# Converting float64 weight slabs in pairs of 1024 columns in a packed-attention and MLP kernel

## The chip, the cores and the metric

One Trainium2 chip, one of its cores. The metric is the device time of one execution, in microseconds (us); the profile's span runs from the first to the last instruction inside it. Engines are named as in the profile: PE is TensorE (PEld its weight loads), DVE is VectorE, ACT is ScalarE, POOL is GpSimd, SP is SyncE, whose queue (SPq) issues almost all DMAs.

## The reference

Three stages in a row, in float32. The inputs arrive as they were drawn, and the weight matrices of the two MLPs arrive as float64.

```python
p_packed = sm_attn(p, k, v)             # 32 packed queries per head, 8 x 8 heads, 576 keys, width 64
out = sm_attn(q, p_packed, p_packed)    # 576 queries on 32 packed rows
x = transposed to (4608, 512)
xn = x / rms * rms_g
x = (silu(xn @ w_gate) * (xn @ w_val)) @ w_out      # 512 -> 1536 -> 512
h = x @ w_in
y = np.maximum(0.01 * h, h) @ w_out2                # 512 -> 2048 -> 512
```

## The kernel before, in words

**Three stretches.** The head (the slots with negative numbers in the tables) does the attention of the first two batches. Then 96 steps of the first MLP follow: a step is one group of 256 hidden columns (six groups), one of two batches of a pair and one half of the batch's 576 tokens. A step runs the products g and v (line 924, `gv`), the SiLU and its product with v (line 938, `hidden`), and four products y of the step before it (line 947, `y_out`). The attention of later batches, weight conversions and other small work hang between them in slots, four to a step. At last the second MLP runs in five blocks of tokens by a fast product scheme (seven products in place of eight, twice over); its weights and their sums lie in DRAM by then.

**Weights.** PE takes each matrix as two parts, a rounded one and the rest of it (hi and lo), so each product is three matmuls. The gate and value weights are first multiplied with the packed attention rows by `fold` (line 883): four small matmuls per batch into a PSUM tile `pwps`, a copy of it on ACT (hi, `pw`, line 170) and a subtraction on DVE (lo, line 178). The next g and v products read `pw`.

**Conversion.** A float64 slab of 128 rows and 512 columns is made float32 by `convert` (line 694): an absolute value on ACT (line 704), then on DVE a clamp (707), a shift (713), the sign bits (724) and the low word (730). All of it runs on raw words. For the 24 slabs of gate and value weights (named `w`) the result stays as it is. For the 12 slabs of `w_out` (named `wo`, the intermediate `cvwo`) and the 32 of the second MLP (`w2`, the intermediate `cvw`) an ACT copy and a POOL subtraction split it into hi and lo. That is 68 conversions. Each converted slab is also stored to DRAM for the later batch pairs, by a store that is issued when the next conversion has been written (`flush_store`).

**Buffers.** `raw_tile` (line 773) holds raw slabs. The tag `wraw` (the slabs `w` and later `w2`) and the tag `w2` (the slabs `wo`) have two buffers each, one slab per buffer. Slabs `w2`, `w3` and `wo1` borrow room from tiles that are not yet in use. The intermediates have two buffers (`CVB`). The SP instruction that loads a slab is issued when the slab that was in its buffer has been read by line 730.

**Order.** The tables ONE, TWO, SPLITW, SPLITO, FOLD0, FOLD, SPLITA and WARM give each piece of work a slot. The conversions of the second MLP start at step 25 and come every 1.6 steps. The framework then sets the order on every engine by its own simulated timeline; what stands in an engine's queue runs in that order, and an instruction that has to wait holds all behind it.

Of the kernel before, what the change touches and what calls it, by code (L numbers as in the profile page):

```python
# [59 lines left out]
SPLITA = (-18, -20,)  # L60
WBUFS = 8
HEAD = 2
OWN = 1
HOLD = 2
# [5 lines left out]
CVB = 2  # L70
# [4 lines left out]
WARM = ([-85, 5], [-53, 2], [-41, 10], [-22, 1],)  # L75
# [3 lines left out]
def pack_attention_moe_kernel(  # L79
# [21 lines left out]
    P = 128  # L101
# [24 lines left out]
    w_dram = dram.tile([NFG * KT, P, 512], F32, name="w_dram")  # L126
# [567 lines left out]
    def convert(raw64, hl, name, whole=False, lay=None, plain=None):  # L694

        hiw, low = raw64[:, :, 1], raw64[:, :, 0]
        n = raw64.shape[1]
        st = {}

        def begin():  # L700
            c = st["c"] = (
                hl if whole else cvt.tile([P, n], F32, tag="conv", bufs=CVB, name="cv" + name)
            )
# [24 lines left out]
        def tail():  # L728
# [47 lines left out]
    NW = NFG * KT  # L776

    def load_w(i):
        if i < NW:
            fg, kt = i // KT, i % KT  # L780
            if i in (2, 3):
                t = mlpa.tile([P, 2, 512, 2], U32, tag="pw1", bufs=2, name=f"w{i}")[:, 0]
            else:
                t = raw_tile(f"w{i}")
            for x, w in enumerate((w_gate, w_val)):
                nc.sync.dma_start(
                    out=t[:, x * G * P : (x + 1) * G * P, :].rearrange("p f w -> p (f w)"),
                    in_=w[kt * P : kt * P + P, fg * G * P : (fg + 1) * G * P].bitcast(U32),
                )
# [23 lines left out]
    def load_wo(i):  # L813
        if i < NF1:
            if i == 1:
                t = mlpa.tile([P, 2, 512, 2], U32, tag="pw0", bufs=2, name=f"wo{i}")[:, 0]
            else:
                t = raw_tile(f"wo{i}", "w2")
            nc.sync.dma_start(
                out=t.rearrange("p f w -> p (f w)"), in_=w_out[i * P : i * P + P, :].bitcast(U32)  # L820
            )
            wo["r", i] = t

    def split_wo(i):
        if i < NF1:
            until(lambda: ("r", i) in wo)
            t = mlpb.tile([P, 2, 512], F32R, tag="wo", bufs=4, name=f"wo{i}")
            convert(wo.pop(("r", i)), t, f"wo{i}")

            def done():  # L830
                wo["s", i] = t
                flush_store()
                stores.append((wo_dram[i], t))
                if i >= 1:
                    load_wo(i + 1)

            after(done)
        elif i < NPAIR * NF1:
            t = mlpb.tile([P, 2, 512], F32R, tag="wo", bufs=4, name=f"wo{i}")
# [647 lines left out]
```

## Time and profile before

| | |
|---|---|
| median of 3 runs | 1608.43 us (1606.33 to 1608.69) |
| the profiled execution | 1609.27 us |
| its span | 1607.5 us |
| PE busy | 1533.7 us (95%) |
| DVE busy | 1115.1 us (69%), 2026 instructions |
| ACT busy | 762.5 us (47%), 1390 instructions |
| POOL busy | 600.3 us (37%) |
| mean granted TensorE clock | 0.985 |

Shares of busy time are means over stretches that differ much: PE is busy for 83 of the first 120 us, for 200 of the next 210, and nearly all of the last 700. So the views by stretch, the waits and the chain that ended last say more than the table. A matmul that reads a PSUM or SBUF tile late shows as idle time of PE with the engine that released it.

### The profile page before, as it was taken

Reading aid. Unit: us, or ns where it says so; the run is one execution under the profiler, and the core shown is the slowest. Engines: PE = TensorE matmul, PEld = TensorE weight load, DVE = VectorE, ACT = ScalarE, POOL = GpSimd, SP = SyncE. Lnnn points to the kernel's source line nnn. Section 1 sums busy time; section 2 is a strip of 40 time slices with the busy share of each in tenths; the row PEclk is TensorE's granted clock in tenths of the full one; section 3 lists DMA queues with packets and bytes.
Section 4 is the critical chain, followed back from the end, with each engine's and each line's share of the span. In section 5 each row is a group of like instructions: output and inputs, shape, how many; then the busy total and the mean of one; then the engine's idle time right before and its main releaser. Section 6 shows DMA issues by size and latency. Waiting matters only on the chain.

```text
span 1607.5 us, 29455 instructions
## 1 busy us (share of the span) xinstructions
PE 1533.7 (95%) x10754; PEld 1353.8 (84%) x10754; DVE 1115.1 (69%) x2026; ACT 762.5 (47%) x1390; POOL 600.3 (37%) x415
## 2 busy tenths in 40 slices
PE   4789999999999999999999999999999999999998
PEld 3558778888888888898999988888888888888998
DVE  7787997566766757879667549646854783596475
ACT  3365454464445554456434246336524652463453
POOL 1124334443524524365124463065208503710530
PEclk7999999999999999999999999999999999999999
DMA  9664562375556744559775666797787769777887
GB/s 273 211 196 148 186 206 88 129 237 176 185 190 210 246 144 148 201 181 351 244 249 207 228 203 203 212 291 203 203 260 241 206 201 288 203 202 227 279 252 209
DMA packets 219455, 342.22 MB, mean 213 GB/s; under 512 B 21168, under 2 KB 120496, under 8 KB 219312
## 3 DMA queue, kind: packets, MB, share of 16 engines
q1 hardware_dynamic: 199856, 330.90, 65.2%
q10 hardware_dynamic: 19456, 9.44, 2.2%
q8 instruction: 86, 1.41, 0.4%
q14 instruction: 57, 0.47, 0.1%
HBM read 266.86 MB, written 73.40 MB: 212 GB/s over the span
## 4 chain that ended last, share of the span: by engine, by line
PE 66%; DVE 16%; DMA 8%; ACT 4%; issue 3%; POOL 1%; SPq 1%; ACTq 0%; DVEq 0%; POOLq 0%
PE o L153 21%; PE h L153 20%; PE y L153 10%; PE g L153 5%; PE v L153 5%; DMA w<-in_moe_w_in_dram 3%; DVE y_acc L963 2%; PE pwps L901 1%; DVE sg L940 1%; DVE pw L178 1%; PE xp L577 1%; DMA k<-in_k_dram 1%; DVE cvw L707 1%; PE s L250 1%; DVE cvw L724 1%
## 5 line engine op out<-in xcount | busy, mean ns | idle before, releaser
L153 PE MATMUL o<-gh,pc 128*128 128x480 f32 (+1 forms) x1120 | 322.7, 369 | 0.0
L153 PE MATMUL y<-hh,wo 128*128 128x288 f32 x1536 | 276.3, 302 | 15.2 <-DVE pw L178 7.1
L153 PE MATMUL h<-yh,pc 128*128 128x480 f32 (+1 forms) x1120 | 278.3, 369 | 0.8 <-DVE y_acc L963 0.5
L153 PEld LDWEIGHTS y<-hh,wo 128*128 128x128 f32 x1536 | 225.4, 190 | 42.4 <-DVE pw L178 9.4
L178 POOL TENSOR_TENSOR hl<-sg,hh 128x576 fp32r<-128x576 f32 x96 | 147.1, 1533 | 299.4 <-ACT hh L170 267.1
L153 PEld LDWEIGHTS h<-yh,pc 128*128 128x128 f32 x1120 | 207.5, 188 | 27.5 <-issue 0.9
L153 PEld LDWEIGHTS o<-gh,pc 128*128 128x128 f32 x1120 | 208.6, 188 | 26.0
L178 DVE TENSOR_TENSOR gl<-g,gh 128x480 fp32r<-128x480 f32 (+1 forms) x280 | 178.9, 657 | 63.5 <-ACT gh L170 56.9
L170 ACT ACTIVATE gh<-g 128x480 fp32r<-128x480 f32 (+1 forms) x280 | 160.5, 587 | 128.8 <-PE o L153 72.8
L153 PE MATMUL o<-gl,pc 128*128 128x480 f32 (+1 forms) x560 | 206.3, 369 | 0.0
L1311 POOL TENSOR_TENSOR b6h<-b6h,b5h 128x480 f32<-128x480 f32 (+1 forms) x40 | 59.2, 1481 | 354.2 <-ACT b5h L170 267.7
L963 DVE TENSOR_TENSOR y_acc<-y_acc,y 128x288 f32<-128x288 f32 x320 | 139.4, 446 | 66.3 <-PE y L153 65.3
L153 PE MATMUL y<-hl,wo 128*128 128x288 f32 x768 | 165.2, 298 | 1.0 <-POOL hl L178 1.0
L153 PE MATMUL h<-yl,pc 128*128 128x480 f32 (+1 forms) x560 | 161.5, 369 | 0.0
L153 PE MATMUL g<-ath,pw 128*128 128x288 f32 x768 | 150.9, 306 | 3.7 <-ACT sg L1251 3.4
L153 PE MATMUL v<-ath,pw 128*128 128x288 f32 x768 | 148.6, 305 | 4.6 <-DVE sg L940 4.6
L153 PEld LDWEIGHTS g<-ath,pw 128*128 128x128 f32 x768 | 115.9, 188 | 24.9 <-issue 10.5
L153 PEld LDWEIGHTS y<-hl,wo 128*128 128x128 f32 x768 | 124.8, 191 | 2.3 <-POOL hl L178 2.3
L1305 POOL TENSOR_TENSOR g<-g,g 128x480 f32<-128x480 f32 (+1 forms) x80 | 117.0, 1462 | 23.9 <-ACT g L1295 18.8
L153 PEld LDWEIGHTS v<-ath,pw 128*128 128x128 f32 x768 | 117.0, 190 | 10.2 <-DVE sg L940 6.5
L153 PEld LDWEIGHTS o<-gl,pc 128*128 128x128 f32 x560 | 105.1, 188 | 13.1
L153 PEld LDWEIGHTS h<-yl,pc 128*128 128x128 f32 x560 | 104.3, 188 | 13.1
(162 smaller groups left out, 2443.9 us busy)
## 6 DMA issues: line engine op xcount, KB each, us to landing
pc<-s_dram SPq DMA_DIRECT2D x320, 256.0 KB, 3.0
pc<-w_dram SPq DMA_DIRECT2D x240, 256.0 KB, 3.0
w<-w_dram SPq DMA_DIRECT2D x72, 256.0 KB, 4.1
wo<-wo_dram SPq DMA_DIRECT2D x36, 512.0 KB, 5.2
w_dram<-w2s SPq DMA_DIRECT2D x32, 512.0 KB, 4.8
s_dram<-ss SPq DMA_DIRECT2D x32, 512.0 KB, 6.3
v<-in_v_dram SPq DMA_DIRECT2D x16, 576.0 KB, 5.2
y_dram<-y_acc SPq DMA_DIRECT2D x32, 288.0 KB, 2.5
```

Source lines behind the costliest of these rows:

```text
L153: mm = nc.tensor.matmul(ps, lhsT=lh if a == "h" else ll, rhs=rh if b == "h" else rl, start=start and i == 0, stop=stop and i == n - 1,)
L170: nc.scalar.activation(out=o, in_=i, func=AF.Copy, scale=scale)
L178: eng.tensor_tensor(out=o, in0=a, in1=hi.bitcast(F32), op=ALU.subtract)
L250: nc.tensor.matmul(t[:, k_, :CH], lhsT=left[:, j].rearrange("p h k -> p (h k)"), rhs=right[:, c * CS : (c + 1) * CS, j, :], start=j == 0, ...
L577: nc.tensor.matmul(xp[:, k_, :CH], lhsT=Pm[:, 2 * x : 2 * x + 2, :].rearrange("p h d -> p (h d)"), rhs=st["AT"][:, c * CS : (c + 1) * CS, ...
L707: nc.vector.tensor_scalar(out=c, in0=c, scalar1=DBL_MIN, scalar2=DBL_MAX, op0=ALU.max, op1=ALU.min)
L724: nc.vector.scalar_tensor_tensor(out=cu, in0=hiw, scalar=0xC0000000, in1=cu, op0=ALU.bitwise_and, op1=ALU.bitwise_or)
L901: return nc.tensor.matmul(ps[32 * h : 32 * h + 32], lhsT=lpw[2 * (n // NFG) + bb][rs, 2 * u + h // 2, c : c + 32], rhs=w[h // 2][rs], star ...
L940: nc.vector.tensor_tensor(out=hf, in0=sg, in1=vps[:, :, :CH], op=ALU.mult)
L963: pace[:] = [nc.vector.tensor_tensor(out=ya, in0=ya, in1=pv, op=ALU.add).ins]
L1305: eng.tensor_tensor(out=o, in0=a, in1=b, op=ALU.subtract)
L1311: return eng.tensor_tensor(out=o, in0=a, in1=b, op=ALU.add)
```

## The change

Two slabs are converted as one: 34 conversions of 1024 columns in place of 68 of 512. The raw tile becomes a pair, and each raw tag, the intermediates (`CVB`) and the split tiles of the second MLP keep one buffer of twice the size. So the buffers hold the same bytes, and a load of the next pair with the same tag waits for the last DVE operation on the pair before it, save for the first two pairs of each kind, of which one borrows room as before. The copies to hi and the subtractions to lo stay at 512 columns, two of each for a pair. Loads of `w` and `wo` are the same DMAs as before, in fours and twos; a pair of `w2` comes by one DMA of 1 MB. A pair of gate and value weights is stored and fetched again as one. The tables get new slots; those of the conversions have half as many entries.

```diff
-SPLITW = (-68, -58, -59, -57, -12, -6, -1, -1, 4, 6, 12, 13, 21, 29, 29, 29, 37, 38, 44, 42, 48, 50, 55, 56,)
-SPLITO = (-56, -65, 1, 7, 26, 29, 33, 41, 49, 53, 67, 71,)
-FOLD0 = (-38, -36, 3, -1,)
+SPLITW = (-67, -58, -37, -1, 0, 11, 21, 28, 36, 43, 47, 53,)
+SPLITO = (-56, 2, 26, 34, 49, 67,)
+FOLD0 = (-38, -38, 6, 0,)
-WBUFS = 8
+WBUFS = 4
-HOLD = 2
+HOLD = 1
-CVB = 2
+CVB = 1
...
-    def convert(raw64, hl, name, whole=False, lay=None, plain=None):
-
-        hiw, low = raw64[:, :, 1], raw64[:, :, 0]
-        n = raw64.shape[1]
+    def convert(raw, name, whole=None, halves=()):
+
+        raw = raw.rearrange("p k f w -> p (k f) w")
+        hiw, low = raw[:, :, 1], raw[:, :, 0]
+        n = raw.shape[1]
...
-            if not whole:
-                if lay:
-                    nc.sync.dma_start(out=plain, in_=c)
-                    hi, lo, c = lay(hl, c)
-                else:
-                    hi, lo = hl[:, 0, :], hl[:, 1, :]
-                act_copy(hi, c)
-                sub(nc.gpsimd, lo, c, hi)
+            for k_, (to, plain) in enumerate(halves):
+                ck = c[:, 512 * k_ : 512 * k_ + 512]
+                if plain is not None:
+                    nc.sync.dma_start(out=plain, in_=ck)
+                hi, lo, ck = to(ck)
+                act_copy(hi, ck)
+                sub(nc.gpsimd, lo, ck, hi)
...
-    def raw_tile(name, tag="wraw", bufs=2):
-        return cvt.tile([P, 512, 2], U32, tag=tag, bufs=bufs, name=name)
+    def raw_tile(name, tag="wraw"):
+        return cvt.tile([P, 2, 512, 2], U32, tag=tag, bufs=1, name=name)
...
                 stores.append((w_dram[i], t))
-                if i >= 2:
-                    load_w(i + 2)
+                if i == 0:
+                    load_w(2)
+                elif i >= 2:
+                    load_w(i + 1)
...
+            if i == 0:
+                load_wo(2)
+            elif i >= 2:
+                load_wo(i + 1)
...
     def load_w2(i):
-        if i < 32:
+        if i < 16:
             t = raw_tile(f"w2{i}")
-            nc.sync.dma_start(out=t.rearrange("p f w -> p (f w)"), in_=w2_src(i)[0].bitcast(U32))
+            to = t.rearrange("p k f w -> p k (f w)")
+            nc.sync.dma_start(out=to, in_=w2_src(i).bitcast(U32))
             w2q[i] = t
...
-    for j in range(32):
-        convs.setdefault(CONV0 + int(j * CONV), []).append(j)
+    for j in range(16):
+        convs.setdefault(CONV0 + int(2 * j * CONV), []).append(j)
```

**ACT at the first folds of group 1.** Here `w7` and `w8` before, and `w3` and `w4` in the change (`w3` holds the old `w6` and `w7`, `w4` the old `w8` and `w9`), are the first operations of conversions; `pw` are the hi copies of the folds. Before:

```order
L704 ACTIVATE w7_726<-w7_694 128x512
L584 ACTIVATE sq011_804<-xp011_0_805 128x288
L584 ACTIVATE sq011_804<-xp011_1_806 128x288
L704 ACTIVATE w8_837<-w8_723 128x512
L170 ACTIVATE pw01_736<-pwps001_811 128x512
L170 ACTIVATE pw11_849<-pwps101_850 128x512
L170 ACTIVATE pw10_847<-pwps100_848 128x512
```

And in the change:

```order
L584 ACTIVATE sq011_782<-xp011_0_783 128x288
L584 ACTIVATE sq011_782<-xp011_1_784 128x288
L170 ACTIVATE pw11_810<-pwps101_811 128x512
L170 ACTIVATE pw10_808<-pwps100_809 128x512
L170 ACTIVATE pw11_810<-pwps111_833 128x512
L170 ACTIVATE pw10_808<-pwps110_832 128x512
L707 ACTIVATE w4_717<-w4_695 128x1024
```

The conversion that stood ahead of the folds (`w8`) now stands behind all four copies of group 1, and `w7` has gone forward with its pair (`w3`, eleven rows above the first `pw11`).

**DVE ahead of the folds of group 2.** `sg` is the product of the SiLU with v, `pw` the lo part of a fold. Before, with the pair of slabs `w13` and `w14` (`w14` in the second raw buffer):

```order
L730 SCALAR_TENSOR_TENSOR w13_1521<-w13_1111,w13_1521 128x512
L940 TENSOR_TENSOR sg011_1278<-sg011_1278,v011_1288 128x576
L707 TENSOR_SCALAR w14_1531<-w14_1531 128x512
L730 SCALAR_TENSOR_TENSOR cvwo5_1552<-wo5_1438,cvwo5_1552 128x512
L713 TENSOR_SCALAR w14_1531<-w14_1531 128x512
L724 SCALAR_TENSOR_TENSOR w14_1531<-w14_1308,w14_1531 128x512
L730 SCALAR_TENSOR_TENSOR w14_1531<-w14_1308,w14_1531 128x512
L178 TENSOR_TENSOR pw21_1346<-pwps201_1347,pw21_1346 128x512
```

And in the change, where `w6` is the old `w12` and `w13`, and `w7` the old `w14` and `w15`:

```order
L733 SCALAR_TENSOR_TENSOR w6_1239<-w6_987,w6_1239 128x1024
L727 SCALAR_TENSOR_TENSOR cvwo2_1378<-wo2_285,cvwo2_1378 128x1024
L968 TENSOR_TENSOR sg011_1216<-sg011_1216,v011_1226 128x576
L733 SCALAR_TENSOR_TENSOR cvwo2_1378<-wo2_285,cvwo2_1378 128x1024
L710 TENSOR_SCALAR w7_1424<-w7_1424 128x1024
L716 TENSOR_SCALAR w7_1424<-w7_1424 128x1024
L178 TENSOR_TENSOR pw21_1286<-pwps201_1287,pw21_1286 128x512
```

Three operations stand between the last one on the pair `w6`, which frees the only raw buffer, and the first one on the pair `w7`, which is loaded into it.

**ACT among the conversions of the second MLP.** `w2s` is the hi copy at the end of a conversion, `cvw` the absolute value that begins one. Before:

```order
L170 ACTIVATE w2s6_4771<-cvw26_4772 128x4x128
L584 ACTIVATE sq141_4841<-xp141_0_4842 128x288
L584 ACTIVATE sq141_4841<-xp141_1_4843 128x288
L170 ACTIVATE lpw5_4852<-tp50_4849,g_sb_115 128x64 x2
L704 ACTIVATE cvw28_5163<-w28_5002 128x512
```

And in the change:

```order
L170 ACTIVATE w2s5_5357<-cvw25_5358 128x4x128 x2
L1279 ACTIVATE sg1011_5499<-g1011_5478 128x576
L170 ACTIVATE hh1010_5431<-sg1010_5395 128x576
L170 ACTIVATE e160_5451<-s160_1_5454 128x9x32
L170 ACTIVATE e160_5451<-s160_0_5453 128x9x32
L707 ACTIVATE cvw26_5674<-w26_5372 128x1024
```

In both, the load that the `cvw` row reads is issued when DVE has done the last operation of the conversion whose `w2s` copy stands first; the number of operations between is four in both, and the change has two copies of 512 columns in front of them.

## Rows read from the trace of the kernel before

**Rows 1.** Busy time by stretch: us, PE, PEld, DVE, ACT, POOL, clock, DMA share, GB/s.

```profile
0.00:120.00 120.00, 83.00 (x608) 60.38 (x608) 93.16 (x180) 55.42 (x101) 22.80 (x25) 0.89 0.74 226
80.00:120.00 40.00, 32.71 (x240) 23.95 (x238) 33.62 (x60) 26.28 (x47) 10.15 (x7) 1.00 0.61 196
120.00:330.00 210.00, 199.82 (x1894) 174.31 (x1900) 162.96 (x327) 105.39 (x185) 88.63 (x60) 0.98 0.48 154
330.00:750.00 420.00, 405.22 (x3747) 360.68 (x3731) 303.19 (x594) 218.80 (x383) 180.37 (x127) 0.99 0.60 200
900.00:1608.00 708.00, 699.47 (x3360) 620.54 (x3360) 444.20 (x727) 318.76 (x596) 260.56 (x176) 1.00 0.77 231
```

**Rows 2.** Chain that ended last, in two windows of the head: start, us, what.

```profile
37.29 7.58 DMA k<-in_k_dram
44.95 4.63 DMA wo<-in_moe_w_out_dram
...
by line: DMA w<-in_moe_w_val_dram 12.6%; DVE w L730 10.7%; DVE w L724 9.6%; issue 8.3%; DVE pw L178 7.2%; DVE w L713 6.4%; PE y L153 6.1%; DVE qT L497 5.1%; DVE sg L940 5.1%; DVE sm L536 4.8%; PE s L250 3.8%; PE g L153 3.0%; PE xp L577 2.9%
96.63 3.28 DMA w<-in_moe_w_val_dram
```

**Rows 3.** PE waits, 330 to 750 us: for whom, us in total, times, longest.

```profile
PE y L153 <- DVE pw L178: 6.1, 7, 2.2
```

**Rows 4.** ACT waits for raw slabs of the second MLP, 330 to 750 us.

```profile
ACT cvw L704 <- DMA w<-in_moe_w_in_dram: 37.2, 12, 5.5
ACT cvw L704 <- DMA w<-in_moe_w_out_dram: 22.3, 11, 3.9
```

**Rows 5.** DVE in order of time, independent operations: start, us.

```profile
133.25 0.42 DVE L707 TENSOR_SCALAR cvwo<-cvwo 128x512 f32<-128x512 f32 x1
133.59 0.42 DVE L707 TENSOR_SCALAR w<-w 128x512 f32<-128x512 f32 x1
136.53 0.68 DVE L724 SCALAR_TENSOR_TENSOR cvwo<-wo,cvwo 128x512 uint32<-128x512 uint32 x1
137.13 0.68 DVE L724 SCALAR_TENSOR_TENSOR w<-w,w 128x512 uint32<-128x512 uint32 x1
139.54 0.75 DVE L940 TENSOR_TENSOR sg<-sg,v 128x576 f32<-128x576 f32 x1
```

**Rows 6.** All engines in order of time, one conversion whose operations follow each other.

```profile
98.24 0.69 DVE L724 SCALAR_TENSOR_TENSOR w<-w,w 128x512 uint32<-128x512 uint32 x1
98.97 0.69 DVE L730 SCALAR_TENSOR_TENSOR w<-w,w 128x512 uint32<-128x512 uint32 x1
100.10 0.43 SPq L786 DMA_DIRECT2D w<-in_moe_w_val_dram  x1
```

**Rows 7.** Groups by form: busy us, mean ns of one | idle before.

```profile
L343 DVE STREAM_TRANSPOSE kT<-k 128x1152 f32<-128x1152 f32 x16 | 21.6, 1348 | 4.7 <-DMA k<-in_k_dram 4.7
L551 DVE STREAM_TRANSPOSE AT<-A 128x576 f32<-128x576 f32 x16 | 12.3, 770 | 4.9 <-POOL A L542 4.6
L704 ACT ACTIVATE cvw<-w 128x512 f32<-128x512 f32 x32 | 21.5, 672 | 63.7 <-DMA w<-in_moe_w_in_dram 37.2 <-DMA w<-in_moe_w_out_dram 22.3 <-POOL wo L178 2.4
L170 ACT ACTIVATE w2s<-cvw 128x512 fp32r<-128x512 f32 x32 | 20.2, 631 | 36.1 <-DVE cvw L730 35.7
L178 POOL TENSOR_TENSOR wo<-cvwo,wo 128x512 fp32r<-128x512 f32 x12 | 15.9, 1328 | 34.2 <-ACT wo L170 34.2
```

**Rows 8.** All engines in order of time, 30 to 51 us.

```profile
30.75 1.51 PE L422 MATMUL pp<-v,a1T 96*32 96x64 f32 x48 [3.32 <-DMA v<-in_v_dram]
37.95 0.47 DVE L430 SCALAR_TENSOR_TENSOR Pm<-pp,rin,mask 128x256 f32<-128x256 f32 x1
50.37 0.43 DVE L707 TENSOR_SCALAR cvwo<-cvwo 128x512 f32<-128x512 f32 x1 [2.83 <-ACT cvwo L704]
```

**Rows 9.** DMA issues: KB each, median us to landing; windows 88 to 330 and 330 to 750 us.

```profile
w<-in_moe_w_val_dram SPq DMA_DIRECT2D x17, 256.0 KB, 3.5
w<-in_moe_w_in_dram SPq DMA_DIRECT2D x14, 512.0 KB, 4.9
```

More of the change, by code (lines that the diff above doesn't have):

```diff
@@ L701, in begin @@
             c = st["c"] = (
[L702 removed]
+                cvt.tile([P, n], F32, tag="conv", bufs=CVB, name="cv" + name)
+                if whole is None
+                else whole.rearrange("p k f -> p (k f)")
             )
@@ L771, in until @@
             drain(1)
-    def raw_tile(name, tag="wraw", bufs=2):
-        return cvt.tile([P, 512, 2], U32, tag=tag, bufs=bufs, name=name)
-    NW = NFG * KT
+    def raw_tile(name, tag="wraw"):
+        return cvt.tile([P, 2, 512, 2], U32, tag=tag, bufs=1, name=name)
+    NW = NFG * KT // 2
     def load_w(i):
         if i < NW:
-            fg, kt = i // KT, i % KT
-            if i in (2, 3):
-                t = mlpa.tile([P, 2, 512, 2], U32, tag="pw1", bufs=2, name=f"w{i}")[:, 0]
+            fg, k0 = i // 2, i % 2 * 2
+            if i == 1:
+                t = mlpa.tile([P, 2, 512, 2], U32, tag="pw1", bufs=2, name=f"w{i}")
             else:
                 t = raw_tile(f"w{i}")
[L785 to L789, printed above, removed]
+            for k_ in range(2):
+                kt = k0 + k_
+                for x, w in enumerate((w_gate, w_val)):
+                    nc.sync.dma_start(
+                        out=t[:, k_, x * G * P : (x + 1) * G * P, :].rearrange("p f w -> p (f w)"),
+                        in_=w[kt * P : kt * P + P, fg * G * P : (fg + 1) * G * P].bitcast(U32),
+                    )
             wq["r", i] = t
@@ L813, in load_wo, with wo_tile, done, fetch_wo @@
     def load_wo(i):
-        if i < NF1:
+        if i < NF1 // 2:
             if i == 1:
-                t = mlpa.tile([P, 2, 512, 2], U32, tag="pw0", bufs=2, name=f"wo{i}")[:, 0]
+                t = mlpa.tile([P, 2, 512, 2], U32, tag="pw0", bufs=2, name=f"wo{i}")
             else:
                 t = raw_tile(f"wo{i}", "w2")
-            nc.sync.dma_start(
-                out=t.rearrange("p f w -> p (f w)"), in_=w_out[i * P : i * P + P, :].bitcast(U32)
-            )
+            for k_ in range(2):
+                m = 2 * i + k_
+                nc.sync.dma_start(
+                    out=t[:, k_].rearrange("p f w -> p (f w)"),
+                    in_=w_out[m * P : m * P + P, :].bitcast(U32),
+                )
             wo["r", i] = t
+    def wo_tile(i):
+        return mlpb.tile([P, 2, 512], F32R, tag="wo", bufs=4, name=f"wo{i}")
     def split_wo(i):
[L825 to L831, printed above, removed]
-                flush_store()
[L833 to L839, printed above, removed]
+        until(lambda: ("r", i) in wo)
+        ts = [wo_tile(2 * i + k_) for k_ in range(2)]
+        halves = [((lambda c, t=t: (t[:, 0, :], t[:, 1, :], c)), None) for t in ts]
+        convert(wo.pop(("r", i)), f"wo{i}", halves=halves)
+        def done():
+            for k_, t in enumerate(ts):
+                wo["s", 2 * i + k_] = t
+                flush_store()
+                stores.append((wo_dram[2 * i + k_], t))
+            if i == 0:
+                load_wo(2)
+            elif i >= 2:
+                load_wo(i + 1)
+        after(done)
+    def fetch_wo(i):
+        if i < NPAIR * NF1:
+            t = wo_tile(i)
             ins = nc.sync.dma_start(out=t.bitcast(F32), in_=wo_dram[i % NF1])
@@ L862, in load_w2, with done @@
     def load_w2(i):
-        if i < 32:
+        if i < 16:
             t = raw_tile(f"w2{i}")
-            nc.sync.dma_start(out=t.rearrange("p f w -> p (f w)"), in_=w2_src(i)[0].bitcast(U32))
+            to = t.rearrange("p k f w -> p k (f w)")
+            nc.sync.dma_start(out=to, in_=w2_src(i).bitcast(U32))
             w2q[i] = t
     def split_w2(i):
-        if i < 32:
-            until(lambda: i in w2q)
-            t = cvt.tile([P, 1024], F32R, tag="w2", bufs=2, name=f"w2s{i}")
-            convert(w2q.pop(i), t, f"w2{i}", lay=by_unit if i < 16 else by_block, plain=w2_src(i)[2])
-            def done():
+        until(lambda: i in w2q)
+        t = cvt.tile([P, 2, 1024], F32R, tag="w2", bufs=1, name=f"w2s{i}")
+        by = by_unit if i < 8 else by_block
+        halves = [((lambda c, k_=k_: by(t[:, k_], c)), w2_at(2 * i + k_)[1]) for k_ in range(2)]
+        convert(w2q.pop(i), f"w2{i}", halves=halves)
+        def done():
+            for k_ in range(2):
                 flush_store()
-                stores.append((w2_src(i)[1], t))
-                load_w2(i + 1)
-            after(done)
+                stores.append((w2_at(2 * i + k_)[0], t[:, k_]))
+            load_w2(i + 1)
+        after(done)
     pw = {}
@@ L885, in fold @@
             return
-        ks = [n * KT + 2 * u + x for x in range(2)]
-        until(lambda: all(("s", k_) in wq for k_ in ks))
-        w = [wq["s", k_] for k_ in ks]
+        k_ = 2 * n + u
+        until(lambda: ("s", k_) in wq)
+        w = [wq["s", k_][:, x] for x in range(2)]
         outs = []
@@ L989, in pack_attention_moe_kernel @@
     nc.sync.dma_start(out=g_sb, in_=rms_g.rearrange("(k p) -> p k", p=P))
-    weights = [lambda i=i: load_w(i) for i in range(4)]
+    weights = [lambda i=i: load_w(i) for i in range(2)]
     weights += [lambda: load_wo(0), lambda: load_wo(1)]
```

31 lines of the change are left out of this document (19 added, 12 removed), and 36 rows, old and new, of tables (ONE, TWO).

## The prediction

> **What bounds the kernel now.** I read the busy time by stretch first, then the chain of waits in the head, then who waits for whom, and last single durations. By stretch [rows 1], PE is idle for 120 − 83.0 = 37.0 us of the first 120, of which 40 − 32.7 = 7.3 us lie in the last 40; for 210 − 199.8 = 10.2 us of the next 210; for 420 − 405.2 = 14.8 us from 330 to 750; and for 8.5 us of the last 708, in which there are no conversions. The clock is at its upper level nearly everywhere after the head (0.98 to 1.00), so there is little of it to win back. PE is the bound from 120 us on, and a change to DVE and ACT work can give at most what PE idles: some 10 and 15 us in the two middle stretches, and a part of the head's 37. DVE is nearly full only in the head (93.2 of 120 us); from 330 to 750 us it is busy for 303 of 420, so a shorter DVE queue there is worth something only where PE or ACT waits for it.
>
> In the head the chain goes through DMA and the conversions. Between 82 and 108 us the four DVE and DMA entries of `w` hold 12.6 + 10.7 + 9.6 + 6.4 = 39.3% of 26 us, that is 10.2 us, and the DMA that lands at about 99.9 us is the raw half of one late slab [rows 2]. From 330 to 750 us PE's largest wait is for the lo part of a fold, which stands behind conversions in DVE's queue (6.1 us in 7 waits) [rows 3]. ACT waits for the raw slabs of the second MLP 12 times for 37.2 us and 11 times for 22.3 us, 59.5 us in all [rows 4].
>
> **What a wide operation costs.** 68 × 4 = 272 DVE operations become 34 × 4 = 136, and 68 ACT ones 34. Columns stay the same, so only the fixed part of 136 DVE operations goes. Independent clamps of 512 columns start 133.59 − 133.25 = 0.34 us apart, independent sign operations 137.13 − 136.53 = 0.60 [rows 5]; two that depend on each other 98.97 − 98.24 = 0.73 apart [rows 6]. Two transposes give a slope: (1348 − 770) / (1152 − 576) = 1.00 ns a column [rows 7], so 512 columns are 0.51 us. Of the sign operation that leaves 0.60 − 0.51 = 0.09 independent and 0.73 − 0.51 = 0.21 dependent. For the clamp, with its own steeper speed, I have no slope. I take 0.13 us an operation, nearer to the independent end because the scheduler mixes other work in; the ends are 0 and 0.21. In sum 136 × 0.13 = 17.7 us of DVE time: 7 pairs before 120 us (28 operations, 3.6 us), 11 pairs up to 330 us (44, 5.7 us), 16 pairs of the second MLP (64, 8.3 us). One sign operation of 1024 columns is then 0.69 + 0.51 = 1.20 us. The absolute value on ACT (0.67 us [rows 7]) becomes 1.1 us as an estimate, between 0.67 (all of it fixed) and 1.35 (twice), nearer to the upper end, as the columns weigh most in the DVE rows too. The Trainium skill, "Perfetto Trace Analysis", section "Optimizing Scalar/DVE Operations", puts the data access of a DVE operation on SBUF at about 60 ns; by that the saving would be an estimated 136 × 0.06 = 8.2 us, under what the pitches here give, and the sum below would gain some 2 us less.
>
> **The head, up to 120 us.**
> 1. *The start.* `Pm` starts at 37.95 us, 5.7 us after its product ended (30.75 + 1.51 = 32.26) [rows 8], since DVE is still on conversions. 25 narrow operations stand ahead of it before, 11 wide ones (22 narrow ones' worth) now: two clamps and one sign operation less (2 × 0.41 + 0.68 = 1.5 us) and 11 × 0.13 = 1.4 us of fixed cost: −2.9. Against it, the first fetch of `wo` is twice as large: 0.5 MB at the 226 GB/s of the stretch [rows 1] is 2.2 us more of DMA ahead of later loads. That is on the path only if `k`, which takes 7.58 us there [rows 2], comes later than DVE wants it. I take −2.9; ends −2.9 and −0.7.
> 2. *wo.* DVE stands still for 2.83 us at 50.37 for ACT, which waits for a raw slab of `wo` (4.63 us on the chain) [rows 2, 8]. This slab is now part of a pair converted later, so the wait goes, and a 1.20 us operation stands ahead of the softmax sums in its place. With one intermediate, the next conversion waits for ACT copy (0.63), two POOL subtractions (2 × 1.33) and the absolute value (1.1) [rows 7], 4.4 us against some 3.1 us of other DVE work: a new stall of 1.3. Net 1.20 + 1.3 − 2.83 = −0.3; ends −2.8 (the new stall covered, the wide operation behind the sums) and +1.5 (the wait had other cover).
> 3. *The fifth slab.* Its four operations (2 × 0.42 + 2 × 0.68 = 2.2 us [rows 5]) go from slot −12 forward to slot −37, out of the end of the first attention, where DVE and PE take turns on the chain: half, −1.0; ends 0 and −2.2.
> 4. *82 to 108 us.* Of the 10.2 us of `w` on the chain, the late slab's DMA and operations go: one pair, loaded long before, stands there. But PE idles only 7.3 us from 80 to 120 us [rows 1], and what is late next are the folds' products and `sg`, in the same chain: −3; ends 0 and −6.
>
> Head: −2.9 − 0.3 − 1.0 − 3.0 = −7.2.
>
> **120 to 330 us.** 5.7 us of DVE time go. PE idles 10.2 of the 210 us, and a third of the relief reaches it: −2. Against it, each kind now has one raw buffer: the load of the next pair of `w` is issued behind the last operation on the pair before. Four SP issues (0.43 each [rows 6], 1.5 to the last), 3.5 us to land [rows 9] and 1.1 us on ACT are 6.1 us; where the new order shows three operations between (two wide sign ones and `sg`, 1.20 + 1.20 + 0.75 [rows 5] = 3.15), DVE stalls for 3 us, and the lo parts `pw` of the second group stand behind it, for which PE waits. At one more place, between `w3` and `w4`, some 1.3 us are missing by the same count. Elsewhere the slots leave more room than the load needs. The first is felt in full, the second not, since no fold stands right behind it: +3, so net +1; ends −6 (no stall felt, all relief felt) and +9. On ACT, `pw` of group 1 loses one narrow absolute value ahead of it, 0.67 us, and gets none; I cost that at nothing, since DVE's part comes later than ACT's.
>
> **330 to 750 us.** 32 loads of 512 KB become 16 of 1 MB. A load was issued with one hi copy and four other operations between it and the ACT operation that reads it; now two copies (2 × 0.63 [rows 7]) and four. Landing took 4.9 us [rows 9]; another 0.5 MB at 200 GB/s [rows 1] makes about 7.5 at most, so less two copies and the other four operations (some 4 us), one wait is 1 to 3 us, 15 of them about 30 us: half of the 59.5 goes. PE felt 14.8 / 59.5 = 0.25 of ACT's waits at most, so 0.25 × 30 = 7.4; a part of its idle time there is for other engines, so I take −4; ends −10 (this and 8.3 us of DVE relief by a third) and +6. The intermediate's single buffer costs nothing here, because the conversions are 3.2 steps apart: that cover goes only if a load is later than a step.
>
> POOL's subtractions, ACT's copies, PE's products and the bytes of all DMAs stay; the last 708 us stay: 0.
>
> **Sum.** 1609.27 − 7.2 + 1 − 4 = 1599.1, so 1599. The profiled execution (1609.27, span 1607.5) is 0.84 above the median of three, 1608.43, against which the result counts; I don't correct for so little.
>
> **The rivals.**
> *R1, slower: the single raw buffers show their loads.* Every reuse of the `w` buffer stalls DVE by up to 3.1 us: 7 × 3.1 = 21.7, less the relief of 5.7, is 16, half of it felt: B = +8. ACT waits 15 × 4.9 = 73.5 us in place of 59.5, a quarter felt: +3.5. The head gives −4. Sum 1609.3 − 4 + 8 + 3.5 = 1617. It decides where the work between the last operation on a pair and the first on the next is over 3 us shorter than the load at more than three places. For it: ACT already waits on these loads with two buffers [rows 4]. Against: the order shows that only at two places of `w`. The Trainium skill, "Trainium Kernel Development and Optimization", section "Best Practices", tells to double-buffer so that DMA lies beside compute, and so speaks for this rival.
> *R2, no change: other work is late next.* The first loads are DMA-bound, so the head gives −2 and the middle stretches nothing: 1607. For it: `k` and `wo` on the chain by 7.58 and 4.63 us [rows 2], DMA busy for 0.74 of the head [rows 1].
> *R3, the change doesn't do what it says:* the fixed cost is hidden and a wide operation takes as long as two narrow ones. Head −1.5 − 0.5 − 1 − 2 = −5, then +3 and −4: 1603. For it: independent clamps overlap to 0.34 us [rows 5].
> *R4, all of it felt:* −7.2, −5 and −8: 1589. The skill's section on DVE operations says that where an engine is not saturated but leaves gaps on others, smaller instructions may finish work sooner; by that rule this rival fails, and the 303 of 420 us in [rows 1] fit its condition.
>
> **Numbers.** The forecast 0.45 (its own range 1592 to 1605), R1 0.18, R2 0.12, R3 0.15, R4 0.10. Slower by over 0.2% (3.2 us, about what a measurement of this kernel can tell from no change): R1, 0.18; within: R2, 0.12; faster: the rest, 0.70. The range runs from 1587, R4 less 2 us, to 1612, which takes in R1 where it costs only half of its terms; outside are some 0.13 of R1 and 0.05 below R4.
>
> **What would show it.** Right: clamps and sign operations of 1024 columns at about 0.7 and 1.20 us, DVE busy some 18 us less; no DVE wait for `cvwo` near 50 us; the chain from 82 to 108 us without a raw `w` DMA; the ACT waits for slabs of the second MLP near 30 us. Wrong: DVE idle in front of `w` clamps for over 5 us between 120 and 330 us, PE idle there above 13 us, ACT waits for the second MLP above 60 us, or the head's PE idle time still near 37 us.

## The result and the profile after

The changed kernel takes 1624.77 us, median of 4 runs (1621.68 to 1632.22), against 1608.17 before (median of 4): a ratio of 1.0112 with a 95% interval of 1.0077 to 1.0147. Two later measurements beside other kernels gave 1.0094 (1.0067 to 1.0120) and 1.0103 (1.0084 to 1.0123). So it is slower by 1.1%, where 0.6% faster was forecast. The profiled execution took 1621.68 us, its span 1619.9: 12.4 us more than before.

The view by stretch of the changed kernel, which answers to [rows 1], has the same columns: us, PE, PEld, DVE, ACT, POOL, clock, DMA share, GB/s.

```profile
0.00:120.00 120.00, 84.08 (x601) 61.29 (x602) 84.91 (x141) 48.46 (x83) 19.85 (x24) 0.83 0.68 209
80.00:120.00 40.00, 34.00 (x242) 25.01 (x241) 27.76 (x38) 19.93 (x36) 7.67 (x6) 0.91 0.34 108
120.00:330.00 210.00, 188.84 (x1777) 163.70 (x1776) 152.87 (x278) 103.40 (x171) 84.62 (x54) 0.97 0.47 155
330.00:750.00 420.00, 405.67 (x3774) 360.50 (x3772) 282.52 (x531) 218.89 (x369) 187.67 (x132) 1.00 0.59 197
900.00:1608.00 708.00, 706.52 (x3422) 627.70 (x3420) 454.61 (x738) 320.62 (x599) 263.56 (x178) 1.00 0.78 232
```

The added idle time of PE has one place. From 120 to 330 us it idles 210 − 188.84 = 21.2 us in place of 10.2, and gets 1777 products done in place of 1894. From 330 to 750 us it idles 14.3 us in place of 14.8. In the first 120 us it idles 35.9 us in place of 37.0, but at a granted clock of 0.83 in place of 0.89. DVE did get its relief: 1089.6 us busy in place of 1115.1, 136 operations less. Work that DVE was spared did not reach PE.

Two products, the same ones of both kernels, show where the lag begins. In the kernel before, from PE's rows in order of time:

```profile
116.32 4.04 PE L602 MATMUL ms<-sq,ones 128*128 128x288 f32 x16
127.83 0.88 PE L422 MATMUL pp<-v,a1T 96*32 96x64 f32 x48
```

In the changed kernel, chosen rows of SP, DVE, ACT and PE in order of time (start, us; what ended the idle time before stands in brackets):

```profile
112.08 1.23 DVE L733 SCALAR_TENSOR_TENSOR w<-w,w 128x1024 uint32<-128x1024 uint32 x1
113.37 0.33 SPq L790 DMA_DIRECT2D w<-in_moe_w_gate_dram  x1
114.69 0.43 SPq L790 DMA_DIRECT2D w<-in_moe_w_val_dram  x1
117.77 4.04 PE L602 MATMUL ms<-sq,ones 128*128 128x288 f32 x16
120.45 1.14 ACT L707 ACTIVATE w<-w 128x1024 f32<-128x1024 f32 x1 [5.38 <-DMA w<-in_moe_w_val_dram]
124.25 0.69 ACT L170 ACTIVATE y_acc<-y 128x288 f32<-128x288 f32 x2
124.70 1.33 PE L153 MATMUL y<-hh,wo 128*128 128x288 f32 x4 [2.35 <-ACT y_acc L170]
134.04 1.13 ACT L707 ACTIVATE w<-w 128x1024 f32<-128x1024 f32 x1 [5.40 <-DMA w<-in_moe_w_val_dram]
135.08 0.67 ACT L170 ACTIVATE hh<-sg 128x576 fp32r<-128x576 f32 x1
135.80 0.80 PE L153 MATMUL y<-hh,wo 128*128 128x288 f32 x4 [2.96 <-ACT hh L170]
136.53 0.88 PE L422 MATMUL pp<-v,a1T 96*32 96x64 f32 x48
...
165.48 1.12 ACT L707 ACTIVATE w<-w 128x1024 f32<-128x1024 f32 x1 [5.21 <-DMA w<-in_moe_w_val_dram]
167.24 0.46 DVE L379 TENSOR_REDUCE mx<-s 128x1 f32<-128x288 f32 x1 [3.18 <-ACT e L170]
167.75 0.28 PE L234 MATMUL s<-ones 128*128 128x16 f32 x1 [3.30 <-DVE mx L379]
169.03 2.17 PE L268 MATMUL s<-qT,PT 32*32 32x288 f32 x32 [1.01 <-ACT y_acc L170]
...
200.77 1.12 ACT L707 ACTIVATE w<-w 128x1024 f32<-128x1024 f32 x1 [6.75 <-DMA w<-in_moe_w_val_dram]
202.24 0.75 PE L577 MATMUL xp<-AT,Pm 128*128 128x288 f32 x2 [1.62 <-ACT sqa L584]
```

At `ms` the changed kernel is 117.77 − 116.32 = 1.5 us late, at `pp` 136.53 − 127.83 = 8.7. In between, the last operation on the pair `w4` ends at 113.31; only then can SP issue the four DMAs of `w5` into the one buffer, and ACT can begin `w5` at 120.45, 7.1 us later. ACT has nothing it may do in these 5.38 us, because its queue runs in order and the copies `y_acc` and `hh` stand behind: PE waits for them 2.35 us. The same comes with `w6` (5.40 us, PE 2.96), and later with a copy of attention scores (`e`, 165.48 us) and the squares (200.77 us) behind the stalled operation. These five PE waits are 2.35 + 2.96 + 3.30 + 1.01 + 1.62 = 11.2 us, as much as the 21.2 − 10.2 = 11.0 us by which PE idles more; the rest of its idle time there, 10.0 us, is as much as the kernel before has.

ACT's waits for raw slabs in the changed kernel, `w` from 120 to 330 us, then the second MLP from 330 to 750 us ([rows 4]): us, times, longest.

```profile
ACT w L707 <- DMA w<-in_moe_w_val_dram: 32.6, 7, 6.8
...
ACT cvw L707 <- DMA w<-in_moe_w_out_dram: 22.2, 7, 5.3
ACT cvw L707 <- DMA w<-in_moe_w_in_dram: 13.0, 6, 4.1
```

For `w` it was 8.1 us in the kernel before, by the same view. For the second MLP the sum fell from 59.5 to 35.2 us.

### The profile page after: what moved, and what is told of

Read it like the earlier page. It is cut to its first block, busy times and chain, and to the rows that moved or that the text cites. A ratio compares the mean times of both kernels' runs of the same rounds, so it can differ in the third digit from the quotient of the medians.

```text
span 1619.9 us, 29154 instructions
## 1 busy us (share of the span) xinstructions
PE 1536.5 (95%) x10754; PEld 1354.4 (84%) x10754; DVE 1089.6 (67%) x1890; ACT 759.5 (47%) x1358; POOL 602.0 (37%) x415
## 4 chain that ended last, share of the span: by engine, by line
PE 63%; DVE 9%; DMA 6%; ACT 3%; issue 2%; POOL 1%; SPq 0%; ACTq 0%; DVEq 0%; POOLq 0%
PE o L153 21%; PE h L153 20%; PE y L153 10%; PE g L153 4%; PE v L153 4%; DMA sl<-c_dram 1%; DVE y_acc L991 1%; PE pwps L929 1%; PE xp L577 1%; DVE pw L178 1%; DVE ss L178 1%; DMA w<-in_moe_w_out_dram 1%; DVE sl L1154 1%; DVE cvw L727 1%; DMA w<-in_moe_w_in_dram 1%
## 5 line engine op out<-in xcount | busy, mean ns | idle before, releaser
L178 DVE TENSOR_TENSOR gl<-g,gh 128x480 fp32r<-128x480 f32 (+1 forms) x280 | 184.0, 676 | 65.8 <-ACT gh L170 59.2
L153 PE MATMUL g<-ath,pw 128*128 128x288 f32 x768 | 147.1, 304 | 6.6 <-ACT sg L1279 4.1
```

Of the source, the lines that this page charges most:

```text
L153: mm = nc.tensor.matmul(ps, lhsT=lh if a == "h" else ll, rhs=rh if b == "h" else rl, start=start and i == 0, stop=stop and i == n - 1,)
L178: eng.tensor_tensor(out=o, in0=a, in1=hi.bitcast(F32), op=ALU.subtract)
```

## The experiments

Theory A: the single raw buffer of `w` makes ACT stand in order behind a load that can't start earlier. Rivals: B, the wide operations hold DVE's queue; C, the single intermediate; D, the new slots; E, for what is left, the order of the wide work ahead of `AT` at 97 us. Ratios are to the kernel before on the same chip, with 95% intervals.

**two_w.** Two raw buffers, and loads a pair earlier.

```diff
-        return cvt.tile([P, 2, 512, 2], U32, tag=tag, bufs=1, name=name)
+        return cvt.tile([P, 2, 512, 2], U32, tag=tag, bufs=2 if tag == "wraw" else 1, name=name)
...
-                elif i >= 2:
-                    load_w(i + 1)
+                elif i == 2:
+                    load_w(3)
+                if i >= 2:
+                    load_w(i + 2)
```

> The changed kernel with two raw buffers for the pairs of w, and the load of pair i+2 issued behind pair i (from the third on). Theory A (ACT stands in order behind the raw load of w, because the one buffer lets it start only after the pair before): ACT's waits for w between 120 and 330 us fall from 32.6 us to under 10, PE idle time there falls by 8 to 11 us, the time goes from 1624.8 to 1611 to 1616. Theory B (wide operations block DVE's queue) and theory C (the single intermediate): under 3 us of change, 1622 or more.

1620.06 us, 1.0068 (1.0048 to 1.0087): better than the change, less than expected (1611 to 1616), and the intervals of the two overlap a little. The raw waits went as theory A says, and for the second MLP too, which has the same tag; from 120 to 330 us PE idles 14.2 us in place of 21.2. ACT's waits for `w` from 120 to 330 us, then all its waits for `cvw` from 330 to 750 us, and the view of that stretch:

```profile
ACT w L707 <- DMA w<-in_moe_w_val_dram: 6.5, 3, 3.0
...
ACT cvw L707 <- POOL w2s L178: 11.2, 10, 1.8
ACT cvw L707 <- DMA c_dram<-cvw: 1.3, 2, 0.8
...
330.00:750.00 420.00, 407.94 (x3788) 362.21 (x3787) 284.87 (x533) 223.97 (x376) 188.55 (x133) 0.99 0.58 197
```

In the second stretch none of the 35.2 us of raw waits is left. ACT stands for POOL's subtractions and for stores of the single intermediate in their place, and all its waits there sum to 198.4 us, 201.1 in the change. PE idles 12.1 us in place of 14.3: 35 us of raw waits were worth 2 us of PE. But the framework put other work ahead of the first `y` in the head, which starts 6.6 us after that of the kernel before, where the change is 1.3 us late. The run shows what the waits were, not what their removal alone is worth.

**late_w.** One buffer; the conversions stand later.

```diff
-SPLITW = (-67, -58, -37, -1, 0, 11, 21, 28, 36, 43, 47, 53,)
+SPLITW = (-67, -58, -37, -1, 0, 16, 25, 34, 42, 50, 56, 64,)
```

> One raw buffer as in the changed kernel, but the conversions of w from the sixth pair on stand in later slots (16, 25, 34, 42, 50, 56, 64 in place of 11, 21, 28, 36, 43, 47, 53), so that their load has landed when ACT comes to them. Theory A: ACT's waits for w between 120 and 330 us fall to under 12 us and the time to 1612 to 1617. Theories B and C: no change beyond 3 us.

1631.01 us, 1.0140 (1.0119 to 1.0161), slower than the change: a miss. The raw waits only halved (16.8 us), and went elsewhere. Rows of PE, ACT and DVE in order of time:

```profile
129.40 0.88 PE L422 MATMUL pp<-v,a1T 96*32 96x64 f32 x48
...
208.53 1.12 ACT L707 ACTIVATE w<-w 128x1024 f32<-128x1024 f32 x1 [7.21 <-DMA w<-in_moe_w_val_dram]
210.28 0.46 DVE L379 TENSOR_REDUCE mx<-s 128x1 f32<-128x288 f32 x1 [3.33 <-ACT e L170]
210.79 1.96 PE L929 MATMUL pwps<-w,lpw 64*32 64x512 f32 x16 [6.21 <-DVE mx L379]
```

Where the wait is gone, the loss is gone: `pp` is late by 129.40 − 127.83 = 1.6 us in place of 8.7. Where a raw wait of 7.21 us comes up later, ahead of the copy of scores `e`, PE stands for 6.21 us. Slots set the order, not the moment at which a buffer comes free.

**narrow_ops.** The pair's buffers and slots, each operation as two of 512 columns.

```diff
-            first_op = nc.scalar.activation(out=c, in_=hiw.bitcast(F32), func=AF.Abs)
+            for x in hs:
+                first_op = nc.scalar.activation(out=c[:, x], in_=hiw[:, x].bitcast(F32), func=AF.Abs)
```

(and so for the four operations of DVE)

> The buffers, loads and slots of the changed kernel, but each of the five operations of a conversion made as two of 512 columns. Theory B: the time goes back to about 1610. Theory A: ACT still waits some 30 us for w between 120 and 330 us; the time stays at 1622 to 1632 (136 more DVE operations add 0 to 6 us).

1644.25 us, 1.0221 (1.0197 to 1.0245). Theory B's forecast fails: narrow operations don't bring the time back, they cost 1% more, over the range of A too; from 330 to 750 us PE idles 420 − 394.71 = 25.3 us in place of 14.3. ACT's raw waits for `w` from 120 to 330 us are 24.7 us. How much of the added time is the 136 fixed parts and how much the order of DVE's rows, which moved too, stays open. A rule of the Trainium skill speaks for B: page "Perfetto Trace Analysis", section "Optimizing Scalar/DVE Operations", says that smaller instructions may finish work sooner where an unsaturated engine causes gaps elsewhere. This run does not agree with it, though it changed the order along with the width.

**cvb2.** `CVB = 2` in place of 1, nothing else.

> The changed kernel with two intermediates of 1024 columns in place of one. Theory C: 5 us or more come back, under 1620. Theory A: within 3 us of the changed kernel, 1622 to 1628, with ACT's waits for w unchanged at about 32 us.

1634.49 us, 1.0161 (1.0139 to 1.0183): some 10 us over the change by two measurements, so theory C falls. In the head ACT now waited 8.9 us for a raw slab of `wo`, where the change waits for none, and PE 7.6 us for `Pm` in place of 3.2; PE idles 44.1 us of the first 120 in place of 35.9. Theory A missed too: the waits for `w` from 120 to 330 us, expected unchanged, fell to 17.3 us. No theory expected that a second buffer makes it slower.

**b5.** A buffer of its own for the odd pairs from `w5` on.

```diff
-                t = raw_tile(f"w{i}")
+                t = raw_tile(f"w{i}", "wraw2" if i >= 5 and i % 2 else "wraw")
...
+                elif i == 3:
+                    load_w(4)
+                    load_w(5)
+                elif i > 3:
+                    load_w(i + 2)
```

> The changed kernel with one thing more: from w5 on the odd pairs have a raw buffer of their own, and their load is issued a pair earlier; everything up to 99 us stays. Theory A (ACT stands in order behind the raw load of w): ACT's waits for w between 120 and 330 us fall from 32.6 to under 10 us, the PE waits behind them (2.4 us for y_acc and 3.0 us for hh before 140 us, later 3.3, 1.6 and 1.0 us) go, the products of the first group lag before by under 3 us at 130 us in place of 8.7, and the time is 1611 to 1616. Theory D (the new slots or the wide operations are at fault): over 1620.

1629.64 us, 1.0115 (1.0090 to 1.0139): a miss, and its reason is in SP's rows. Since the new buffer was free from the start, the load of `w5` did not stay where it was written but went up beside that of `w2`: eight DMAs of `w` stand there from 33 to 39 us, where the change has four, ahead of `v` (36.03 us in the change) and `k`. A product in the head then waited 7.15 us, 2.6 in the change:

```profile
33.29 0.35 SPq L790 DMA_DIRECT2D w<-in_moe_w_gate_dram  x1
...
38.01 0.43 SPq L790 DMA_DIRECT2D w<-in_moe_w_gate_dram  x1
41.04 0.45 SPq L297 DMA_DIRECT2D v<-in_v_dram  x1
...
59.01 1.33 PE L250 MATMUL s<-kT,pT 128*128 128x288 f32 x2 [7.15 <-ACT sq L584]
```

The raw waits from 120 to 330 us fell to 12.3 us. What that gave, the head had lost: `ms` starts at 123.50 us, 7.2 after the kernel before. "Everything up to 99 us stays" was the wrong part of what was expected.

**old_conv_new_slots.** The kernel before with `ONE`, `TWO`, `FOLD0`, `SPLITA` and `WARM` of the change, and each slot of a pair given to both slabs.

```diff
-SPLITO = (-56, -65, 1, 7, 26, 29, 33, 41, 49, 53, 67, 71,)
+SPLITO = (-56, -56, 2, 2, 26, 26, 34, 34, 49, 49, 67, 67,)
```

> The kernel before, narrow operations and two buffers of one slab, in the slots of the changed kernel (each slot of a pair given to both of its slabs). Theory A: within 4 us of before, 1605 to 1613, since two buffers of one slab leave the loads room. Theory D (the new slots cost the time): 1618 or more.

1637.75 us, 1.0154 (1.0129 to 1.0180): not what theory A expected; the time fits D (1618 or more). With both slabs of a pair in one slot, two buffers of one slab don't give the loads room either: 13 raw waits, 32.9 us, from 120 to 330 us.

**pairs_old_slots.** The change with the slots of the kernel before.

```diff
-SPLITW = (-67, -58, -37, -1, 0, 11, 21, 28, 36, 43, 47, 53,)
+SPLITW = (-68, -58, -12, -1, 4, 12, 21, 29, 37, 42, 48, 55,)
```

(and `ONE`, `TWO`, `FOLD0`, `SPLITA`, `WARM`, `SPLITO`)

> The changed kernel in the slots of the kernel before (a pair takes the slot of its first slab of w, of its later one for the first wo). Theory A: the raw waits of ACT stay (over 25 us between 120 and 330 us), and so does the time, 1620 to 1632. Theory D: 1613 or less.

1657.86 us, 1.0279 (1.0253 to 1.0304), slower than theory A allowed. D falls: the new slots are no cause of the loss, they are worth about 33 us to the pairs (1657.9 − 1624.8, from two measurements). The two runs together say that operations and slots fit only each other.

**w2_pairs_only.** The kernel before with pairs for the second MLP alone.

```diff
-    for j in range(32):
-        convs.setdefault(CONV0 + int(j * CONV), []).append(j)
+    for j in range(16):
+        convs.setdefault(CONV0 + int(2 * j * CONV), []).append(j)
```

(with the `split_w2` and `load_w2` of the change, and buffers of its own)

> The kernel before with pairs for the second MLP alone (16 loads of 1 MB into one raw buffer of their own, wide operations), w and wo as before. The term of the prediction, 4 us gained from 330 to 750 us, would give 1603 to 1606. If ACT's raw waits there lie beside other work (theory A says they do), 1606 to 1611 although they fall from 59.5 to some 35 us. If one buffer costs there too, over 1613.

1644.06 us, 1.0193 (1.0167 to 1.0220). The raw waits of `cvw` from 330 to 750 us fell to 31.8 us, and the time rose. Part of it is again a load that found a free buffer: the first one of the second MLP stood in the head, and ACT waited 13.98 us for it. The rest grew from 330 to 750 us, where PE idles 33.8 us, ACT waits another 24.9 us for late slabs of `w` and `wo`, and the slots were those of narrow conversions. It does not tell what pairs of the second MLP are worth in slots of their own.

**changed_again, second_buffer_held, second_buffer_early.** The change once more, and two ways to give `w` a second buffer without a free load: b5 with the load of `w5` bound behind that of `w4`, and one with the load of each next pair issued when a conversion begins.

```diff
                     load_w(4)
-                    load_w(5)
+                    with tc.issue_after(last_dma[0].ins):
+                        load_w(5)
```

```diff
+            if i >= 3:
+                with tc.issue_after(sp_last[0].ins):
+                    load_w(i + 1)
...
+                t = raw_tile(f"w{i}", "wraw2" if i >= 4 and i % 2 == 0 else "wraw")
```

> The changed kernel unaltered, beside the two that follow on the same chip: 1620 to 1632.

> The changed kernel with a raw buffer of its own for the odd pairs of w from w5 on, as in b5, but the early load of w5 is bound behind the load of w4 in SP's queue, so that it can't go into the first 60 us, where b5's load went and where b5 lost 6 us. Theory A (ACT stands in order behind the raw load of w): the head stays as in the changed kernel (lag behind the kernel before under 2.5 us at the first y), ACT's waits for w from 120 to 330 us are under 12 us, the lag at 130 us is under 4 us in place of 8.7, and the time is 5 to 10 us under the changed kernel. Theory D (new slots and wide operations): not more than 3 us under it.

> Two raw buffers for w from w4 on, each load issued when the conversion of the pair before it begins, bound behind the last load of the attention in SP's queue. Theory A: ACT's waits for w after 100 us under 8 us; 6 to 11 us under the changed kernel, and if the rest of the loss is the slots' that much over the kernel before. Theory D: not more than 3 us under the changed kernel.

On one chip: 1625.49 (1.0094), 1617.80 (1.0047; 1.0027 to 1.0067) and 1628.84 us (1.0114; 1.0088 to 1.0140). The held one's time is what theory A expected, 7.7 us under the change; the two intervals meet only at 1.0067. Its raw waits for `w` from 120 to 330 us are 13.7 us, 35.9 in changed_again (under 12 were expected), and PE idles 15.7 us there in place of 24.8. Its `pp` starts at 131.36 us, 3.5 after the kernel before; that of changed_again at 139.20, 11.4 after. The early one took nearly all raw waits away (5.0 us from 120 to 330 us), and PE idles only 11.6 us there, yet it gained nothing: its sequence put two wide conversions side by side ahead of `AT` in DVE's queue. PE waited 6.82 us for `AT`, 4.67 in the change, and its clock was granted at 0.61 and 0.66 in the two stretches of 10 us behind, between the levels of 1.2 and 2.4 GHz (0.81 and 1.00 in the change). So E is real there. From 330 to 750 us PE idles 20.2 us besides, 14.6 in changed_again; that stays open.

**third_buffer_held, third_buffer_late, held_w3_later.** A third buffer (A, B, C in turn from `w4` on), the same in the slots of late_w, and second_buffer_held with `w3` and `w4` two slots later. The first against second_buffer_held; the load of `w6` is also bound behind that of `w5`:

```diff
-                t = raw_tile(f"w{i}", "wraw2" if i >= 5 and i % 2 else "wraw")
+                t = raw_tile(f"w{i}", ("wraw", "wraw2", "wraw3")[max(i - 4, 0) % 3])
...
-                    load_w(i + 2)
+                    load_w(i + 3)
```

> second_buffer_held with a third raw buffer for the pairs of w from w4 on, loads of w5 and w6 bound behind that of w4: only four instructions of ACT's and PE's queues stand elsewhere than there. Theory A: ACT's waits for w from 120 to 330 us fall from 13.7 to under 6 us, and the time falls by 1 to 5 us more, to 1612 to 1617. Theory E (the rest of the loss is the order of the work, as the product xp waits 4.7 us for AT behind the wide conversion of w3 at 97 us and PE's clock falls): no more than 1 us.

> third_buffer_held with the later slots of late_w (16, 25, 34, 42, 50, 56, 64). Theory A: raw waits already gone, so the slots change the time by under 3 us. Theory E: the work goes to other places, 5 us or more either way.

> second_buffer_held with the conversions of w3 and w4 two and two slots later (1 and 2 in place of -1 and 0), so that less of w3 stands in DVE's queue ahead of AT. Theory E: the wait of xp for AT at 97 us falls from 4.7 to under 3 us, and the lag behind the kernel before at the first y stays under 1 us, but the folds of group 1, which read w3, come later; the time goes down by 1 to 3 us if AT decides, up by 2 to 5 us if the folds do.

On one chip: 1614.88 us, 1.0016 (1.0001 to 1.0032); 1620.83, 1.0053 (1.0034 to 1.0072); 1615.77, 1.0018 (1.0003 to 1.0034). With three buffers the time is back to within 0.3% of before. ACT's waits for raw slabs of `w` from 120 to 330 us, second_buffer_held first:

```profile
ACT w L707 <- DMA w<-in_moe_w_val_dram: 13.7, 4, 5.5
```

and third_buffer_held:

```profile
ACT w L707 <- DMA w<-in_moe_w_val_dram: 3.7, 1, 3.7
```

The two profiles differ by 1 us of span (1615.1 and 1614.1), so the step from two to three buffers is small, while that from one to two is not. The later `w3` shortens the longest wait for `AT` from 4.7 to 4.1 us only, where E needed under 3, and the waits for `w` fell to 3.7 us with it: this run does not tell E from A. The later slots cost 6 us once the loads have room, where theory A allowed 3, so slots do matter by themselves.

**third_buffer_w3_later, changed_third_time.** Both helps together, and the change beside it.

> third_buffer_held with the conversions of w3 and w4 two slots later, both helps together. Theory A: at best what is left of the raw waits (5.9 us after the first 60 us in third_buffer_held) goes, 1 to 3 us: 0 to 0.2% over the kernel before. If it came under the kernel before by 0.2%, the wide conversion would pay once its loads have room; if it stays over it, the 25 us of DVE time that it saves are worth nothing here.

> The changed kernel unaltered beside it, on the same chip: 0.7 to 1.3% over the kernel before, and so over third_buffer_w3_later.

1614.60 us, 1.0035 (1.0023 to 1.0048), and 1624.86, 1.0103 (1.0084 to 1.0123), on one chip: 0.7 of 1.0% comes back, and the time is like that of the third buffer alone (1614.88). The stretch from 120 to 330 us of the first:

```profile
120.00:330.00 210.00, 197.01 (x1898) 171.24 (x1897) 151.62 (x285) 103.54 (x176) 92.74 (x58) 0.99 0.42 140
```

No wait of ACT for `w` is left in it, and 1898 products are done in it as against 1777 in the change and 1894 before. Its `pp` starts at 131.10 us, 3.3 us after that of the kernel before, and its span is 3.2 us longer: in these two executions what is left arises before 131 us. There PE idles less than before (35.3 us in place of 37.0), but at a granted clock of 0.83 in place of 0.89. One such place lies behind the wait for `AT`, 2.98 us before, 4.67 in the change and 4.62 here. The stretch behind it, in the same order (columns as above):

```profile
97.00:103.00 6.00, 4.76 (x47) 1.67 (x47) 4.72 (x9) 3.02 (x7) 0.46 (x1) 1.00 0.70 228
97.00:103.00 6.00, 4.32 (x22) 1.97 (x22) 2.64 (x3) 0.89 (x3) 0.00 (x0) 0.50 0.38 110
97.00:103.00 6.00, 4.41 (x24) 2.04 (x24) 0.78 (x1) 0.98 (x3) 0.63 (x1) 0.50 0.70 245
```

PE is busy about as long, but at half the clock, the lower of its two levels of 1.2 and 2.4 GHz, and gets half the products done. So E may well be a part of what is left; no run took this wait away. No version came under the kernel before. The saved DVE time, 25 us, shows nowhere in the time.

## Why the prediction was wrong

The direction was wrong: −9.3 us forecast, +16.6 measured. Its rival R1, with a chance of 0.18 and 1617 us, had the mechanism, the single raw buffer, but saw it on DVE. Three of its signs of being wrong came: DVE idle in front of `w` clamps for 10.5 us from 120 to 330, PE idle there for 21.2, and the head's PE idle time still near 37 (35.9).

1. *What a wide operation costs:* right for the single operations. Undisturbed, the clamp takes 0.69 us (0.7 forecast), the sign operation 1.22 (1.20), the absolute value 1.13 (1.1). DVE is busy 25.5 us less; the 17.7 forecast were too few.
2. *The head:* −7.2 forecast, at the products `ms` it is +1.5. PE's idle time fell by 1.1 us only, and the forecast had no term for its clock, which was granted at 0.83 in place of 0.89. The wait behind `Pm` shrank by 3.0 us as step 1 said, and no wait for `cvwo` is left at 50 us. But `v` and `AT` are late next, as R2 has it. Waits of PE up to 120 us, before:

```profile
PE tp L464 <- DVE Pm L430: 6.2, 1, 6.2
PE xp L577 <- DVE AT L551: 4.6, 2, 3.0
PE pp L422 <- DMA v<-in_v_dram: 6.5, 2, 3.3
```

and in the change:

```profile
PE tp L464 <- DVE Pm L430: 3.2, 1, 3.2
PE xp L577 <- DVE AT L551: 6.0, 3, 4.7
PE pp L422 <- DMA v<-in_v_dram: 8.1, 2, 4.8
```

The three sums are 17.3 us in both. In step 4 the conversion at 89.74 us waits for no raw slab, as forecast, but the next one, at 107.72 us, does for 2.00 us, and `AT` came to stand behind a wide pair there.
3. *120 to 330 us:* this step failed, +1 forecast and 11 us of added PE idle time measured. Its sentence was "Elsewhere the slots leave more room than the load needs". It counted the operations between two pairs on DVE, at the two places with few rows, and did not ask where ACT's first operation of the next pair stands in ACT's queue. From the last operation to ACT's start the trace shows 7.1 us (6.1 forecast), and at seven places ACT comes to it earlier. The one stall that it priced, DVE's at the second folds, came (4.38 us at 153.88, 3 forecast), but PE did not feel it, where the forecast had it felt in full: the trace shows no wait of PE from 145 to 164 us. second_buffer_held and third_buffer_w3_later, each beside the change on one chip, show the cause: 0.5 of 0.9% and 0.7 of 1.0% came back.
4. *330 to 750 us:* the waits of ACT fell to 35.2 us (some 30 forecast), but PE's idle time only from 14.8 to 14.3. The step that failed is the quarter of ACT's waits that PE was said to feel: in two_w all 35.2 us of raw waits went and PE idled 2.2 us less, a sixteenth, since ACT then waited for other work.

One rule of the Trainium skill spoke for R1: page "Trainium Kernel Development and Optimization", section "Best Practices", tells to double-buffer so that DMA lies beside compute. The runs with two and three buffers agree with it, 32.6 us of raw waits becoming 13.7 and 3.7; b5 and cvb2 show its limit, as a free buffer also lets work in at a place where it costs more.

What stays open: the last 0.2 to 0.4%, for which the clock behind `AT` is the one lead, untested, and why wide operations gain nothing even with room. An order tuned for them might differ; it was not tried.

## What to carry to other kernels

Two buffers made into one of twice the size hold the same bytes but lose the lead: take the time from the last read to the first use of the next load (here 7 us), and find in the queue of the engine that reads first, not of the busiest one, what stands behind that use. A wait is worth what it holds up: 35 us of ACT's raw waits in one stretch cost PE 2 us, 25 us more in another cost it 11. Where a scheduler places loads by itself, a new buffer needs a bound on how early its load may go.

## What was not expected of the hardware

Some DVE operations that run beside one of POOL take longer. Rows of the changed kernel in order of time, first beside POOL's `hl`, then two of a conversion with POOL at rest:

```profile
95.13 1.63 POOL L178 TENSOR_TENSOR hl<-sg,hh 128x576 fp32r<-128x576 f32 x1 [0.17 <-ACT hh L170]
95.54 2.30 DVE L727 SCALAR_TENSOR_TENSOR w<-w,w 128x1024 uint32<-128x1024 uint32 x1
97.77 0.77 DVE L551 STREAM_TRANSPOSE AT<-A 128x576 f32<-128x576 f32 x1
98.68 2.26 PE L577 MATMUL xp<-AT,Pm 128*128 128x288 f32 x4 [4.67 <-DVE AT L551]
...
108.90 0.69 DVE L710 TENSOR_SCALAR w<-w 128x1024 f32<-128x1024 f32 x1 [2.34 <-ACT w L707]
110.83 1.22 DVE L727 SCALAR_TENSOR_TENSOR w<-w,w 128x1024 uint32<-128x1024 uint32 x1
```

The sign operation takes 2.30 us there in place of 1.22, and `AT` and the product stand behind it. Over the whole kernel the mean of this row is 1.54 us for `w`:

```profile
L727 DVE SCALAR_TENSOR_TENSOR w<-w,w 128x1024 uint32<-128x1024 uint32 x12 | 18.5, 1538 | 0.2
```

The Trainium skill, "SBUF — State Buffer", section "SBUF: two separate sides", says that DVE, in an operation with two SBUF inputs as here, and GpSimd share a pair of ports by a lock: whichever starts first holds it for its whole instruction. The changed kernel's trace agrees in the main. Of its 68 wide sign and low-word operations, 25 overlap one of POOL. The 7 that began first took at most 1.22 us, like the 43 that overlap none (1.18 to 1.23). Of the 18 that began second, 13 took 0.3 to 1.2 us longer, up to 2.46 us in all. The other five were hardly delayed, and why stays open.
